# Linear attention into two feed-forward networks: moving one down product per chunk by a unit, and one tile of output products into the tail

## The chip, the cores and the metric

The program runs on one core of a Trainium2 chip, in one launch. The metric is device time in microseconds (us): the median of several runs. The engines are called as the profile calls them: PE is TensorE (PEld its weight load), DVE is VectorE, ACT is ScalarE, POOL is GpSimd, SP is SyncE, which here issues nearly all DMA transfers. Each engine works through its own instructions in a fixed order; an instruction that waits holds up all that stand behind it on that engine.

## The reference

Three steps, one feeding the next:

```python
for t in range(S):                       # attention: B=4, H=8, S=768, D=48
    state = alpha[:, :, t, :, None] * state + k_t v_t^T
    y[:, :, t] = q_t state
x = y as (3072, 384)
h = x @ w_in                             # first network, (3072, 384) @ (384, 2048)
g = (a0 + a1 h + a2 h^2 + a3 h^3) / (1 + |b0| |h| + |b1| h^2 + 1e-6)
x = g @ w_out                            # (3072, 2048) @ (2048, 384)
h = x @ w_in2                            # second network, (3072, 384) @ (384, 1024)
s = h * softmax(h)
out = (layernorm(s) * g_ln) @ w_out2     # (3072, 1024) @ (1024, 384)
```

All inputs and outputs are float32.

## The kernel before, in words

**Chunks and units.** The sequence is cut into six chunks of 128 steps (512 tokens with the four batches). A chunk is 16 units of the first network, one for each block of 128 of the 2048 hidden features; unit u belongs to chunk u // 16. The loop over u runs through 96 units and four more (`LAG = 4`). In it `m_up(u)` (line 592) makes the up products of a unit, nine matmuls into a PSUM tile `hp` (three buffers), and hands them to a chain on ACT, DVE and POOL that ends in `gh` (ACT, line 625) and `gl` (POOL, line 626), the high and low part of g, with two buffers each. `m_down(u - LAG)` (line 638) follows in the same round and adds that unit's nine down products into three PSUM tiles `x2p`, which collect a whole chunk. After a chunk's last unit ACT copies the three `x2p` tiles out (`x2e`, line 646); the first down product of the next chunk writes the same PSUM tiles. The attention of later chunks (lines 236 to 494) is woven into these rounds.

**The second network** works on 24 tiles of 128 tokens, four to a chunk. For tile s, `n_up` (line 712) makes 18 matmuls into a PSUM tile `h`; DVE and ACT then compute softmax, product and layer norm (lines 731 to 750), and DVE transposes blocks of the result (line 752). After the fourth tile of a chunk `n_turn` (line 762) completes the transposition by 16 transfers issued from SP, called turn transfers below. `n_split(s)` makes the high part (ACT, line 767) and the low part (POOL, or DVE for tiles 0 and 20, line 768) of one transposed tile in one of three places. `n_down(s)` (line 776) makes 24 matmuls into a PSUM tile `op` with two buffers, so tile s uses the buffer of tile s - 2. `n_out(s)` copies `op` on ACT into an SBUF tile `o` (line 785), also with two buffers, and four transfers of 32 rows, called output pieces below, carry it to the result (line 788, SP; for the last tile two of them from ACT).

**The order.** The first four tiles of the second network go into the last chunk of the first. The loop over tiles 4 to 23 then makes one tile's up products and norm, then one earlier tile's split, down products and output, except after the tiles named in `SKIP`; `done` counts the down products made, `cut` the splits, at most `AHEAD = 3` beyond `done`. What is left over goes into a last loop, the tail. Before the change 17 tiles of down products (0 to 16) are made in the loop and 7 in the tail.

```python
        while cut < min(done + AHEAD, (s + 1) // B * B):
            n_split(cut)
            cut += 1
        if s not in SKIP:
            n_out(done, n_down(done))
            done += 1
```

The program's scheduler takes the instructions in this order and settles, from priorities and its own model of durations, the order on each engine; waits between engines are semaphores. A second copy of both networks, for inputs that the fast form can't treat, stands behind a branch and isn't run here.

Of the kernel before, what the change touches and what calls it, by code (L numbers as in the profile page):

```python
# [23 lines left out]
def _run(*gens):  # L24
    for g in gens:
        for _ in g:
            pass
# [3 lines left out]
def kernel(  # L31
# [17 lines left out]
    B, H, S, D = q.shape  # L49
# [4 lines left out]
    NCH = S // CH  # L54
# [7 lines left out]
    LAG = 4  # L62
# [15 lines left out]
    G2 = 3  # L78
    MIX = lambda u: u < 24 and u % 2 == 0
    EARLY = (9, 11, 13, 15)  # L80
    SKIP = (5, 7, 11)
    AHEAD = 3
    LATE = 2
    U2, IDLE = NF1 - 1, (0, NF1 // 2 - 1)
    assert (B, H, D, CH) == (4, 8, 48, 128)
# [57 lines left out]
    def judge(moe_pool):  # L143

        sums = const.tile([128, 1], F32, name="sums")
        row = moe_pool.tile([1, 128], F32, name="row", tag="ft", bufs=2)
        tot = const.tile([1, 1], F32, name="tot")
        nc.vector.tensor_reduce(sums, bad, axis=AX.X, op=ALU.add)
        nc.sync.dma_start(out=row, in_=sums)
        nc.vector.tensor_reduce(tot, row, axis=AX.X, op=ALU.add)  # L150
        nc.vector.tensor_scalar(flag, tot, 0.0, None, ALU.is_gt)

    def network(fast):
# [420 lines left out]
        def x_load(c):  # L574
            for kt in range(KT):
                nc.sync.dma_start(
                    out=x_tile(c)[:, kt].rearrange("p a t -> p (a t)").bitcast(F32), in_=y_d[c][128 * kt:128 * kt + 128, :]
                )
# [50 lines left out]
        def m_down(u):  # L629
            c, f = divmod(u, NF1)  # L630
            n, o = divmod(f, 4)
            if f == 0:
                x2ps[c] = [ps_x2p.tile([128, NTOK], F32, name=f"x2p{d}", tag=f"x2p{d}") for d in range(KT)]
            gh, gl = gts.pop(u)
            hi, lo = wo[n]
            for d in range(KT):
                for w, gg in ((hi, gh), (hi, gl), (lo, gh)):
                    nc.tensor.matmul(  # L638
                        x2ps[c][d], lhsT=w[:, o, 128 * d:128 * d + 128], rhs=gg,
                        start=(f == 0 and w is hi and gg is gh), stop=(f == NF1 - 1 and w is lo),  # L640
                    )
            if f == NF1 - 1:
                for d0, n in ((0, 2), (2, 1)):
                    e = moe_pool.tile([128, 2, NTOK], F32, name="x2e", tag="st", bufs=2)
                    for d in range(n):
                        nc.scalar.activation(e[:, d], x2ps[c][d0 + d], AF.Copy, scale=back if fast else 1.0)  # L646
                    nc.sync.dma_start(out=x2_d[c][:, d0:d0 + n, :], in_=e[:, :n])
                del x2ps[c]
# [14 lines left out]
        def w2_load(nm):  # L663
            src = {"i": w2i_d, "o": w2o_d}[nm]
            n, step = {"i": (KT, 1), "o": (NF2, 4)}[nm]
            for z in range(0, n, step):
                for x, y in enumerate("hl"):
                    nc.sync.dma_start(out=w2[nm + y][:, z:z + step].bitcast(F32), in_=src[:, x, z:z + step])
                    yield
# [12 lines left out]
        def open2():  # L682
            if fast:
                ps_a.__exit__(None, None, None)
            ph2["ps_pool"] = tc.tile_pool(name="ps_e", bufs=1, space=PSUM, side="right", reuse_waits="tile")
            ph2["ps"] = ph2["ps_pool"].__enter__()
            if fast:
                att.__exit__(None, None, None)
            ph2["pool"] = tc.tile_pool(name="w2", bufs=1, side="right", reuse_waits="tile")
            pool = ph2["pool"].__enter__()  # L690
            for nm, dims in (("i", [128, KT, DF2]), ("o", [128, NF2, DM])):
                for y in "hl":
                    w2[nm + y] = pool.tile(dims, F32R, name="w2" + nm + y)
# [3 lines left out]
        def room(n, o, size):  # L697
            if n not in area:
                area[n] = moe_pool.tile([128, GW], F32R if n == 3 else F32, name=f"room{n}", tag=f"g{n}")
            return area[n][:, o:o + size]  # L700
# [56 lines left out]
        def n_turn(c):  # L757
            T = room(c % 2, 0, 4 * DF2).rearrange("p (r x) -> p r x", r=4)
            for qq in range(4):
                L = lnT[4 * c + qq] = room(2, DF2 * ((4 * c + qq) % 6), DF2)  # L760
                for r in range(4):
                    nc.sync.dma_start(out=L[32 * r:32 * r + 32, :], in_=T[32 * qq:32 * qq + 32, r])  # L762

        def n_split(s):
            L = lnT[s]
            hi, lo = (room(3, DF2 * (3 * x + s % 3), DF2) for x in range(2))
            nc.scalar.activation(hi, L, AF.Copy)  # L767
            (nc.vector if s in FASTS else nc.gpsimd).tensor_tensor(lo, L, hi.bitcast(F32), ALU.subtract)  # L768
            lnT[s] = (hi, lo)
# [32 lines left out]
        def chain(*gens):  # L802
            for g in gens:
                yield from g
# [48 lines left out]
        def half_steps(i):  # L853
            gp = a_pe(i)
            gd = chain(a_prep(i + 1), a_move_qk(i + 1) if i + 1 >= NPE else iter(()), a_load(i + 2, ("ra", "rk")) if i + 2 < NH and i + 1 >= NPE else iter(())) if i + 1 < NH else iter(())
            while True:
                with pin(GP):
                    a = next(gp, "end")
                with pin(GS):
                    b = next(gd, "end")  # L860
                    if b != "end":
                        b = next(gd, "end")
                if a == "end" and b == "end":
                    if i + 1 < NH:
                        _run(a_enter(i + 1))
                        if i + 2 < NH and i + 1 < NPE:
                            _run(a_load(i + 2))
                    return
                yield
# [2 lines left out]
        side = iter(())  # L872
        tail = None
        prep = iter(())
        for u in range(NU + LAG):
            c, f = divmod(u, NF1)
            now[0] = u
            if f % (NF1 // 2) == LATE and u < NU:
                _run(side)
                i = 2 * c + 2 + f // (NF1 // 2)  # L880
                side = half_steps(i) if fast and i < NH else iter(())
            if u < NU:
                if f == 0 and c == NCH - 1:
                    if fast:
                        judge(moe_pool)
                    open2()
                    tail = chain(w2_load("i"), n_load(0), w2_load("o"))
                if f == 0 and c and not fast:
                    x_load(c)
                if fast and u < NF1:  # L890
                    if f % 4 == 0:
                        _run(prep)
                        if f:
                            stage["near"] = False
                            stage["bank"] = ""
                        prep = w1_group(f // 4 + 2) if f < 8 else iter(())
                    with later(G1):
                        take(prep, 1)
                m_up(u)
                if fast and u < NF1:  # L900
                    with later(G1):
                        take(prep, 1)
            if u == NU:
                _run(n_load(1))
            take(side, 1)
            if u >= U2 and f % (NF1 // 2) in IDLE:
                stage["bank"] = "at"
                with later(G2):
                    take(split2, 1)
            if tail is not None:  # L910
                _run(split2)
                take(tail, 2)
            if u >= LAG:
                m_down(u - LAG)
            if u - NU + NF1 in EARLY:
                n_tile(EARLY.index(u - NU + NF1))
                if len(EARLY) == B and u - NU + NF1 == EARLY[-1]:
                    n_turn(0)
# [7 lines left out]
        done = 0  # L926
        cut = 0
        for s in range(len(EARLY), NS):
            if s % B == 0 and 1 < s // B + 1 < NCH:
                _run(n_load(s // B + 1))  # L930
            n_tile(s)
            if s % B == B - 1:
                n_turn(s // B)
            while cut < min(done + AHEAD, (s + 1) // B * B):
                n_split(cut)
# [4 lines that stand above are left out]
        while done < NS:  # L940
            while cut < min(done + AHEAD, NS):
                n_split(cut)
# [117 lines left out]
```

## Time and profile before

| | us |
|---|---|
| median of 3 runs | 779.71 |
| lowest, highest | 774.92, 781.45 |
| profiled execution, whole time | 776.87 |
| profiled execution, span of its instructions | 775.0 |
| PE busy | 728.0 |
| DVE busy | 630.4 |
| ACT busy | 535.2 |

The profiled execution took 1.87 us more than its span (776.87 less 775.0), and lies inside the range of the runs. Busy times are sums over stages that have different limits, so a stage is read by itself below. All times of single instructions are counted from the start of the span.

### The profile page before, as it was taken

How to read it: one execution, taken by the hardware profiler on the slowest of the kernel's cores; microseconds unless marked ns; L12 is line 12 of the kernel's file. 1: busy time of each engine (PE TensorE's matmuls, PEld its weight loads, DVE VectorE, ACT ScalarE, POOL GpSimd, SP SyncE). 2: the span in 40 equal slices, each digit the busy share in tenths (PEclk: the TensorE clock that was granted, in tenths of full speed). 3: DMA queues.
4: the chain of work that ended last, by engine and by line, in shares of the span. 5: the costliest groups of instructions: out<-in, count | busy, mean ns of one | idle time of the engine just before them, and what ended most of it. 6: DMA issues, size and time to landing. Idle time of an engine off the chain costs nothing.

```text
span 775.0 us, 13914 instructions
## 1 busy us (share of the span) xinstructions
PE 728.0 (94%) x4976; PEld 605.8 (78%) x4976; DVE 630.4 (81%) x1110; ACT 535.2 (69%) x983; POOL 358.4 (46%) x306
## 2 busy tenths in 40 slices
PE   4676999999999999999999999999999999999996
PEld 3565767788888787778877788888888989988986
DVE  4999999989898989899898966478887788877640
ACT  2245867689878888788878887788965545555541
POOL 3255777777554355434444433332243343452322
PEclk9857899999999999999999999999999999999999
DMA  7995446466837382727554350720025253542653
GB/s 167 253 275 165 107 155 167 146 147 206 204 99 161 122 205 83 172 66 207 137 148 91 124 82 1 296 112 0 1 83 132 89 130 90 132 108 52 140 119 76
DMA packets 87278, 101.74 MB, mean 131 GB/s; under 512 B 34464, under 2 KB 63136, under 8 KB 87200
## 3 DMA queue, kind: packets, MB, share of 16 engines
q1 hardware_dynamic: 87104, 100.67, 48.9%
q8 instruction: 41, 0.67, 0.4%
q14 instruction: 37, 0.30, 0.1%
q10 hardware_dynamic: 96, 0.10, 0.0%
HBM read 60.59 MB, written 27.56 MB: 114 GB/s over the span
## 4 chain that ended last, share of the span: by engine, by line
DVE 30%; PE 18%; ACT 12%; issue 5%; SPq 3%; DMA 3%; POOL 1%; ACTq 0%; DVEq 0%; POOLq 0%
PE x2p L638 6%; PE hp L592 6%; DVE room L752 3%; SPq L762 3%; DVE room L735 2%; DVE p L618 2%; ACT jk L737 2%; PE op L776 2%; DVE hp L622 2%; DVE w L621 2%; DMA room<-room 2%; DVE sm L731 2%; DVE room L750 2%; PE h L712 2%; DVE p L623 2%
## 5 line engine op out<-in xcount | busy, mean ns | idle before, releaser
L592 PE MATMUL hp<-xt,g 128*128 128x512 f32 x864 | 224.1, 401 | 14.8 <-DVE p L616 7.5
L626 POOL TENSOR_TENSOR gl<-p,gh 128x512 fp32r<-128x512 f32 x96 | 130.8, 1362 | 193.9 <-ACT gh L625 107.9
L592 PEld LDWEIGHTS hp<-xt,g 128*128 128x128 f32 x864 | 163.2, 192 | 54.2 <-DVE p L616 7.7
L638 PE MATMUL x2p<-gh,g 128*128 128x512 f32 x576 | 196.9, 395 | 2.0 <-ACT x2e L646 2.0
L638 PEld LDWEIGHTS x2p<-gh,g 128*128 128x128 f32 x576 | 107.9, 188 | 29.1 <-ACT x2e L646 4.7
L638 PE MATMUL x2p<-gl,g 128*128 128x512 f32 x288 | 112.9, 392 | 0.0
L776 PE MATMUL op<-w2oh,room 128*128 128x384 f32 x384 | 101.8, 339 | 1.3 <-ACT room L767 0.7
L768 POOL TENSOR_TENSOR room<-room,room 128x1024 fp32r<-128x1024 f32 x22 | 54.8, 2496 | 101.0 <-ACT room L767 79.0
L621 DVE SCALAR_TENSOR_TENSOR w<-w,co,hp 128x512 f32<-128x512 f32 x84 | 62.0, 738 | 43.5 <-ACT hp L620 42.5
L712 PE MATMUL h<-w2ih,x 128*128 128x512 f32 x288 | 90.7, 394 | 0.0
L599 ACT ACTIVATE p<-hp,co 128x512 f32<-128x512 f32 x96 | 66.0, 687 | 12.3 <-POOL gl L626 12.0
L620 ACT ACTIVATE hp<-ah 128x512 f32<-128x512 f32 x84 | 50.1, 597 | 33.3 <-DVE p L618 32.0
L776 PEld LDWEIGHTS op<-w2oh,room 128*128 128x128 f32 x384 | 70.1, 188 | 3.0 <-ACT room L767 1.0
L600 ACT ACTIVATE w<-ah,co 128x512 f32<-128x512 f32 x96 | 69.4, 724 | 1.7 <-DVE hp L622 1.3
L618 DVE SCALAR_TENSOR_TENSOR p<-p,co,hp 128x512 f32<-128x512 f32 x84 | 61.6, 734 | 9.3 <-ACT p L599 9.0
L597 ACT ACTIVATE ah<-hp 128x512 f32<-128x512 f32 x96 | 56.7, 591 | 16.4 <-PE hp L592 16.0
L776 PE MATMUL op<-w2ol,room 128*128 128x384 f32 x192 | 65.0, 339 | 0.0
L625 ACT ACTIVATE gh<-p 128x512 fp32r<-128x512 f32 x96 | 59.9, 623 | 5.7 <-DVE p L623 2.8
L638 PEld LDWEIGHTS x2p<-gl,g 128*128 128x128 f32 x288 | 54.1, 188 | 11.7 <-issue 0.8
L712 PEld LDWEIGHTS h<-w2ih,x 128*128 128x128 f32 x288 | 53.9, 188 | 11.7
L623 DVE SCALAR_TENSOR_TENSOR p<-p,co,hp 128x512 f32<-128x512 f32 x84 | 61.9, 737 | 1.1
L619 ACT ACTIVATE ah<-w,co 128x512 f32<-128x512 f32 x84 | 60.6, 721 | 1.3
(168 smaller groups left out, 1264.7 us busy)
## 6 DMA issues: line engine op xcount, KB each, us to landing
room<-room SPq DMA_DIRECT2D x96, 128.0 KB, 2.3
qk_d<-qk SPq DMA_DIRECT2D x10, 771.0 KB, 4.1
st<-in_moe_w_in_dram SPq DMA_DIRECT2D x13, 512.0 KB, 4.6
st<-in_moe_w_out_dram SPq DMA_DIRECT2D x16, 384.0 KB, 3.5
qks<-qk_d SPq DMA_DIRECT2D x20, 257.0 KB, 4.4
x<-x_d SPq DMA_DIRECT2D x18, 256.0 KB, 3.1
out_dram<-o SPq DMA_DIRECT2D x94, 48.0 KB, 1.6
ra<-in_alpha_dram SPq DMA_DIRECT2D x44, 96.0 KB, 2.8
```

Of the source, the lines that this page charges most:

```text
L592: last["PE", u] = nc.tensor.matmul(hp, lhsT=w[:, kt, 128 * o:128 * o + 128], rhs=xts[c][:, kt, xx, :], start=(kt == 0 and w is hi and xx = ...
L599: nc.scalar.activation(p, hp, AF.Square, bias=co[:, 7:8])
L600: nc.scalar.activation(w, ah, AF.Square, bias=co[:, 6:7])
L618: nc.vector.scalar_tensor_tensor(p, p, a1, hp, ALU.add, ALU.mult)
L619: nc.scalar.activation(ah, w, AF.Ln, bias=rest)
L621: nc.vector.scalar_tensor_tensor(w, w, rest, hp, ALU.add, ALU.mult)
L623: fin[u] = nc.vector.scalar_tensor_tensor(p, p, a0, hp, ALU.add, ALU.mult)
L625: last["ACT", u] = nc.scalar.activation(gh, p, AF.Copy)
L626: last["POOL", u] = nc.gpsimd.tensor_tensor(gl, p, gh[:].bitcast(F32), ALU.subtract)
L638: nc.tensor.matmul(x2ps[c][d], lhsT=w[:, o, 128 * d:128 * d + 128], rhs=gg, start=(f == 0 and w is hi and gg is gh), stop=(f == NF1 - 1 an ...
L712: nc.tensor.matmul(hp[:, 512 * n:512 * n + 512], lhsT=x2s[c][:, kt, x, CH * b:CH * b + CH], rhs=w2[w][:, kt, 512 * n:512 * n + 512], start ...
L776: nc.tensor.matmul(op, lhsT=x[:, 128 * f:128 * f + 128], rhs=w2[w][:, f, :], start=(f == 0 and x is hi and w == "oh"), stop=(f == NF2 - 1 ...
```

## The change

It has two parts. With `HOLD` the list `held` keeps the down products of the first unit of chunks 2, 3 and 4 back by one round: in that round only the up products are put down, in the next one both down products follow one another. With 15 in `SKIP` no down products are made after tile 15, so from tile 16 on every tile's down products stand one tile later, 16 tiles of them are made in the loop and 8 in the tail. A new inner loop makes the splits that are still due for the chunks before, ahead of the turn transfers that overwrite their source.

```diff
-    SKIP = (5, 7, 11)
+    SKIP = (5, 7, 11, 15)
     AHEAD = 3
+    HOLD = (1, NCH - 1)
...
+        held = []
         for u in range(NU + LAG):
...
             if u >= LAG:
-                m_down(u - LAG)
+                held.append(u - LAG)
+            if not (f == LAG and HOLD[0] < c < HOLD[1]):
+                while held:
+                    m_down(held.pop(0))
...
             n_tile(s)
             if s % B == B - 1:
+                while cut < min(done + AHEAD, s // B * B):
+                    n_split(cut)
+                    cut += 1
                 n_turn(s // B)
```

Eight lines are added ahead of the code named here, so the same instruction has a line number higher by one in the rows of after.

On PE, at the start of chunk 2 (the tile `x2p` has three parts, and `sc` is the attention's; chunks 3 and 4 read alike), there stood:

```order
L592 MATMUL hp<-xt,g_629 128x512 x7
L420 MATMUL sc<-qks 128x128 x8
L592 MATMUL hp<-xt,g_629 128x512 x2
L638 MATMUL x2p_3026<-gh,g_134 128x512
L638 MATMUL x2p_3026<-gl,g_134 128x512
L638 MATMUL x2p_3026<-gh,g_134 128x512
L638 MATMUL x2p_3027<-gh,g_134 128x512
L638 MATMUL x2p_3027<-gl,g_134 128x512
L638 MATMUL x2p_3027<-gh,g_134 128x512
L592 MATMUL hp<-xt,g_629 128x512 x9
```

and now, on PE at the same place:

```order
L593 MATMUL hp<-xt,g_629 128x512 x7
L421 MATMUL sc<-qks 128x128 x8
L593 MATMUL hp<-xt,g_629 128x512 x11
L639 MATMUL x2p_3061<-gh,g_134 128x512
L639 MATMUL x2p_3061<-gl,g_134 128x512
L639 MATMUL x2p_3061<-gh,g_134 128x512
L639 MATMUL x2p_3062<-gh,g_134 128x512
L639 MATMUL x2p_3062<-gl,g_134 128x512
```

The nine up products of the next unit moved ahead of the first down products of the chunk.

On SP, over the last three chunks of the second network (`room` is a turn transfer, `out_dram` an output piece, four to a tile), there stood:

```order
L762 DMA room_6225<-room_6208 32x1024 x16
L788 DMA out_dram<-o 32x384 x16
L762 DMA room_6225<-room_5889 32x1024 x16
L788 DMA out_dram<-o 32x384 x20
L762 DMA room_6225<-room_6208 32x1024 x16
L788 DMA out_dram<-o 32x384 x22
```

and now, on SP at the same place:

```order
L763 DMA room_6225<-room_6208 32x1024 x16
L789 DMA out_dram<-o 32x384 x12
L763 DMA room_6225<-room_5889 32x1024 x16
L789 DMA out_dram<-o 32x384 x19
L763 DMA room_6225<-room_6208 32x1024 x16
L789 DMA out_dram<-o 32x384 x27
```

Counted back from the end (tile 23 has two pieces on SP, the others four), the pieces behind the last 16 turn transfers were those of tiles 18 to 23; now they are the fourth piece of tile 16 and all of tiles 17 to 23.

On ACT, from the last tile's layer norm (lines 745 and 746) to the end, there stood:

```order
L745 ACTIVATE sm<-sm 128x1
L746 ACTIVATE sm<-sm 128x1
L785 ACTIVATE o<-op 128x384 x2
L767 ACTIVATE room_6352<-room_6225 128x1024
L785 ACTIVATE o<-op 128x384
L767 ACTIVATE room_6352<-room_6225 128x1024 x3
L785 ACTIVATE o<-op 128x384 x4
```

and now, on ACT at the same place:

```order
L746 ACTIVATE sm<-sm 128x1
L747 ACTIVATE sm<-sm 128x1
L768 ACTIVATE room_6352<-room_6225 128x1024
L786 ACTIVATE o<-op 128x384 x2
L768 ACTIVATE room_6352<-room_6225 128x1024 x3
L786 ACTIVATE o<-op 128x384 x2
L768 ACTIVATE room_6352<-room_6225 128x1024
L786 ACTIVATE o<-op 128x384 x4
```

Before, these were outputs 17 and 18, split 20, output 19, splits 21 to 23, outputs 20 to 23; now they are split 19, outputs 16 and 17, splits 20 to 22, outputs 18 and 19, split 23, outputs 20 to 23.

## Rows read from the trace of the kernel before

**Rows 1.** The page: span, and busy time of each engine.
```profile
span 775.0 us, 13914 instructions
PE 728.0 (94%) x4976; PEld 605.8 (78%) x4976; DVE 630.4 (81%) x1110; ACT 535.2 (69%) x983; POOL 358.4 (46%) x306
```
**Rows 2.** Windows: length; busy PE, PEld, DVE, ACT, POOL; granted clock, DMA share, GB/s.
```profile
262.00:440.00 178.00, 173.41 (x1418) 137.75 (x1419) 162.28 (x264) 147.65 (x270) 83.27 (x78) 1.00 0.54 142
440.00:565.00 125.00, 124.71 (x718) 102.06 (x717) 88.18 (x135) 103.22 (x183) 39.62 (x34) 1.00 0.26 83
565.00:749.70 184.70, 184.70 (x910) 165.11 (x908) 138.84 (x271) 102.30 (x199) 71.57 (x38) 1.00 0.42 106
```
**Rows 3.** Waits of PE from 200 to 450: total, times, longest, in us.
```profile
PE x2p L638 <- ACT x2e L646: 2.0, 6, 0.5
...
PE hp L592 <- DVE p L623: 0.4, 2, 0.2
```
**Rows 4.** Waits of ACT from 262 to 440 (the longest two of four).
```profile
ACT hp L620 <- DVE p L618: 19.2, 11, 3.2
ACT p L599 <- POOL gl L626: 5.5, 9, 1.0
```
**Rows 5.** Waits of ACT from 450 to 565 (the longest of eight).
```profile
ACT ah L597 <- PE hp L592: 9.5, 9, 3.0
```
**Rows 6.** Timeline of PE, start of chunk 2: start, us, idle before and its releaser.
```profile
261.88 0.50 PE L638 MATMUL x2p<-gh,g 128*128 128x512 f32 x1 [0.43 <-ACT x2e L646]
...
263.07 0.50 PE L638 MATMUL x2p<-gh,g 128*128 128x512 f32 x1 [0.23 <-ACT x2e L646]
```
**Rows 7.** Timeline of PE, end of tile 19's down products to the last matmul.
```profile
749.55 0.34 PE L776 MATMUL op<-w2oh,room 128*128 128x384 f32 x1
750.60 0.45 PE L776 MATMUL op<-w2oh,room 128*128 128x384 f32 x1 [0.71 <-ACT room L767]
...
751.86 0.62 PE L776 MATMUL op<-w2oh,room 128*128 128x384 f32 x2 [0.64 <-DVE room L768]
...
768.39 0.33 PE L776 MATMUL op<-w2oh,room 128*128 128x384 f32 x1
```
**Rows 8.** Timeline of ACT: outputs 18 and 20, and split 20.
```profile
745.68 0.49 ACT L785 ACTIVATE o<-op 128x384 f32<-128x384 f32 x1 [2.76 <-PE op L776]
749.49 1.06 ACT L767 ACTIVATE room<-room 128x1024 fp32r<-128x1024 f32 x1 [3.31 <-DMA room<-room]
...
759.44 0.49 ACT L785 ACTIVATE o<-op 128x384 f32<-128x384 f32 x1 [0.24 <-DMA out_dram<-o]
```
**Rows 9.** Timeline of SP's queue: the last turn transfers and the pieces behind them.
```profile
745.25 10.87 SPq L762 DMA_DIRECT2D room<-room  x16
756.21 13.90 SPq L788 DMA_DIRECT2D out_dram<-o  x22
```
**Rows 10.** Timeline of DVE: a step of tile 15, then steps of tile 23.
```profile
681.42 2.07 DVE L747 TENSOR_TENSOR sm<-sm 128x1 f32<-128x1 f32 x1 [0.50 <-ACT sm L746]
...
741.84 0.15 DVE L744 TENSOR_SCALAR sm<-sm 128x1 f32<-128x1 f32 x1 [1.31 <-ACT jk L737]
742.50 0.16 DVE L747 TENSOR_TENSOR sm<-sm 128x1 f32<-128x1 f32 x1 [0.50 <-ACT sm L746]
...
743.93 1.25 DVE L752 STREAM_TRANSPOSE room<-room 128x1024 f32<-128x1024 f32 x1
```
**Rows 11.** Timeline of POOL: the low part of tile 11.
```profile
681.07 2.40 POOL L768 TENSOR_TENSOR room<-room,room 128x1024 fp32r<-128x1024 f32 x1
```
**Rows 12.** Windows, columns as in rows 2.
```profile
75.90:82.70 6.80, 3.46 (x8) 2.78 (x9) 6.77 (x14) 5.21 (x10) 4.86 (x5) 0.50 0.74 128
```
**Rows 13.** Timeline of PE: nine up products before and after a pause.
```profile
68.30 2.33 PE L592 MATMUL hp<-xt,g 128*128 128x512 f32 x9
...
79.24 3.94 PE L592 MATMUL hp<-xt,g 128*128 128x512 f32 x9 [7.55 <-DVE p L616]
```
**Rows 14.** The page's DMA issues: count, KB each, median us to landing.
```profile
out_dram<-o SPq DMA_DIRECT2D x94, 48.0 KB, 1.6
```

## The prediction

> **What bounds the kernel now.** I read the page first, then windows by stage, then the waits inside each stage, and the timelines at the places that the change touches. The page gives PE 728.0 us of a span of 775.0 [rows 1], but that average hides three stages. From 262 to 440 PE is busy 173.4 of 178 us [rows 2] and yet it isn't what sets the pace: in the waits of ACT no PE appears, the longest are for DVE and POOL [rows 4], so the chain of ACT, DVE and POOL runs behind PE, and PE is held by the buffers that the chain gives back. From 440 to 565 it is the other way: PE is busy 124.7 of 125 us [rows 2] and ACT waits for up products, 9.5 us in nine waits [rows 5]. From 565 to 749.7 PE is busy all of 184.7 us [rows 2]. Beside it the second network's norm runs as a chain of its own on DVE and ACT, a few tiles behind the up products; both streams meet at the end. PE ends tile 19 just after 749.55, waits 0.71 and then 0.64 us for the two halves of tile 20, and has nothing but down products from 751.86 to 768.39 + 0.33 = 768.72 [rows 7]. From there to the end it is 775.0 - 768.72 = 6.28 us of last output, which nothing here changes.
>
> **Part 1, the held down product.** Nothing is added or removed, 27 matmuls change places. At the start of chunk 2 PE waits 0.43 and 0.23 us, because ACT hasn't yet copied out the `x2p` tiles [rows 6]; the six waits of this kind are two at each of the three starts that are changed, 2.0 us in all [rows 3]. Nine up products (2.0 to 2.3 us, [rows 13]) now stand ahead and cover them. That is at most 2.0 us of PE's time. But at chunks 2 and 3 the chain on ACT and DVE sets the pace, and what PE saves there it spends waiting for the next `hp` buffer, except that the moved products also let ACT and DVE take some steps earlier. Chunk 4 starts at about 430, ten us ahead of the stage in which PE has no slack, so most of its 0.66 us should reach the end. The moved up products need an `hp` buffer 2.6 us earlier than before; PE has waited for those 0.4 us in total over 250 us [rows 3], so I bound the loss by 0.4. I take a gain of 1.0, between a loss of 0.4 and a gain of 2.0.
>
> **Part 2, one tile more in the tail: PE's own work.** All up products from tile 16 on stand one tile of down products earlier on PE, and all down products one tile later relative to them. The sum of PE's work ahead of tile 20 is the same, in another order, and PE has no idle time up to 749.7, so it arrives at tile 20 at the same time as before. Up products that come earlier help DVE only where DVE waits for them, and it waits for ACT. So this part gives PE nothing by itself; what it can change is when tile 20 is ready.
>
> **Part 2, the end of the norm's chain.** Let T be the end of the last transposition, before at 743.93 + 1.25 = 745.18 [rows 10]. DVE's own order changed around tiles 15 to 18, where two tiles are now interleaved twice. Each tile alone leaves DVE idle for 1.31 + 0.50 us behind ACT [rows 10], so two interleavings can save at most 2 x 1.81 = 3.6 us. Against it, the splits now fall at other moments of the chain, and a step of DVE that begins inside POOL's subtraction is held until that ends: at 681.42 a step of one element a row, elsewhere 0.16 us, took 2.07 us, to the end of the 2.40 us subtraction that began at 681.07 [rows 10, 11]. One such meeting more costs up to 2.4. So T moves between -3.6 and +2.4; I take -0.5, since following the new order by hand through the four tiles I get a gain of one interleaving and lose most of it to one meeting.
>
> **Part 2, the output pieces behind the turn transfers.** This is the largest term. Before, all pieces of tiles 0 to 17 were issued ahead of the last 16 turn transfers; now the fourth piece of tile 16 and those of 17 stand behind them on SP. The 16 take SP 10.87 us from T + 0.07, and the next piece was issued at 756.21, T + 11.0 [rows 9]. It lands 1.6 us later [rows 14], at T + 12.6. Who waits: output 18 on ACT writes the `o` buffer that this piece still reads (two buffers, tiles 16 and 18 share one). Before, the same kind of wait fell on output 20, 0.24 us at 759.44 [rows 8], where it cost nothing. Behind it on PE: tile 20's first matmul writes the `op` buffer that output 18 has to empty. Before, output 18 ran at 745.68 [rows 8], long ahead; now it runs from T + 12.6 to T + 13.1 (0.49 us, [rows 8]). PE starts tile 20 some 0.06 us later (749.49 + 1.06 = 750.55 on ACT, 750.60 on PE, [rows 7, 8]), at T + 13.2 = 758.4 for T unchanged. The 94 matmuls from 751.86 on took 16.86 us, 0.179 each, so 96 take 17.2 and end at 775.6, against 768.72: **+6.8 us**. The two waits of 0.71 and 0.64 us disappear inside this one and are in the sum. Bounds of the landing: output 20 began 3.2 us after the first of the four pieces that it waited for was issued [rows 8, 9], so one piece takes 1.6 to 3.2 us, and I take the median of its own kind. The pieces are 48 KB. The Trainium skill ("DMA: Bandwidth & Descriptors", Anatomy of one DMA) states for the GpSimd path a fixed cost of about 2.0 us and bytes at 436 GB/s, which is an estimate of 2.1 us by that page; by it the sum would be 0.5 us higher, but the trace has 1.6 for this very transfer and decides.
>
> **The clock after the pause.** PE would then stand idle from tile 19's end (749.7, or a little later) to 758. After the pause of 7.55 us ahead of 79.24 the granted clock was 0.50, the lower level of 1.2 GHz, from 75.9 to 82.7 [rows 12], and nine up products took 3.94 instead of 2.33 us [rows 13]. I add these 1.6 us, between nothing (no fall) and 3.4 (the whole stretch of 6.8 us at half speed falls on work).
>
> **The sum.** 6.8 - 0.5 + 1.6 - 1.0 = +6.9 us. The profiled execution would go from 776.87 to 783.8. The median of the runs shown is 2.84 higher than that execution, so on it the forecast is 779.71 + 6.9 = **786.6 us**, slower by 0.9%. A measurement of this kernel can tell about 1%, 7.8 us, from no change; the forecast lies just inside.
>
> **Rival 1, the pause closes and the change is not slower.** The tile that was left for the tail keeps PE busy until tile 20 is ready. Its price: tile 20 would follow tile 19 at 749.73 and the last 96 matmuls end at 749.73 + 17.2 = 766.9, 1.8 us earlier; with 1.0 to 2.0 from part 1 that is some 2.8 to 3.8 us faster, about 776.5. It decides if the fourth piece of tile 16 lands by 749.1, that is if T comes 8.7 us earlier, or if ACT doesn't wait for it. The order shows the piece behind the transfers, and 3.6 is all that interleaving can save. 4%.
>
> **Rival 2, T comes early and the clock holds.** 6.8 - 3.6 - 2.0 = +1.2, or 780.9. For it speaks that two interleavings are really in the order, against it the meetings with POOL, and the fall of the clock in every long pause at the start. 13%.
>
> **Rival 3, everything falls on the later side.** One more meeting on DVE, no saving (T + 2.4 at most; I take + 1.0), a landing of 2.4, a clock cost of 2.5 and no gain from part 1: 6.8 + 1.0 + 0.8 + 2.5 = +11.1, or 790.8. The turn transfers fill SP for 10.87 us in any case, so nothing here is more than an addition of small terms. 13%.
>
> **How the numbers follow.** The forecast (the blocked piece, with terms near those taken) has 70%. The cases by themselves: rival 1 at 776.5, rival 2 at 780.9, forecast 783.5 to 789.5, rival 3 at 790.8. The range 780.0 to 790.5 leaves out rival 1 and half of rival 3, and some of the spread of the median itself, whose runs reach from 774.92 to 781.45. Slower by over 1% takes rival 3 and a third of the forecast: 0.36. Faster by over 1% isn't reached even by rival 1 at its best: 0.02. The rest, 0.62, is within 1%.
>
> **What would show it.** In the waits of PE in chunks 2 to 4 the wait for `x2e` should be gone, and one for `hp` should have grown. In the last 35 us PE should stand idle 6 to 8 us ahead of tile 20, released by ACT's output 18, and that output in turn by the landing of an output piece, issued on SP right behind the last turn transfers. The clock should read 0.50 in a stretch that begins in that pause. If PE runs through from tile 19 to 20, or is released there by a split as before, the largest term is wrong. If the pause is there and the whole is no slower, part 1 gave more than PE's own waits, and my reading of the stage from 262 to 440 is wrong.

## The result, and the profile after

The changed kernel takes 783.72 us (median of ten runs, 782.53 to 787.53) against 777.36 for the kernel before on the same chip (ten runs, 773.78 to 781.45): ratio 1.0091, 95% interval 1.0068 to 1.0114. It is slower, by 0.9%, as forecast: +6.9 us was forecast, and the ratio gives 0.0091 x 777.36 = 7.1 us (the two medians are 6.4 us apart). The time on record as the forecast, 786.6 us, is 2.9 higher, because it starts from the median of three runs, 779.71, and that of ten is 777.36. The changed kernel's profiled execution took 783.25 us with this span and these busy times; PE's 3.5 us more than in [rows 1] are no more work, it has the same 4976 matmuls.

```profile
span 781.4 us, 13916 instructions
PE 731.5 (94%) x4976; PEld 608.5 (78%) x4976; DVE 630.2 (81%) x1110; ACT 534.2 (68%) x983; POOL 356.8 (46%) x306
```

**Chunks 2 to 4.** The waits of PE from 200 to 450 (total, times, longest), to be held against [rows 3] and against two more lines of before:

```profile
PE u L483 <- DVE xt L471: 1.8, 4, 0.7
PE y L444 <- POOL A L428: 0.9, 2, 0.6
```

and after:

```profile
PE u L484 <- DVE xt L472: 2.1, 4, 0.7
PE hp L593 <- DVE p L624: 1.6, 5, 0.5
PE y L445 <- POOL A L429: 0.9, 2, 0.6
```

The wait for `x2e` is gone (it was 2.0), the wait for an `hp` buffer has gone from 0.4 to 1.6, and that for `xt` from 1.8 to 2.1. All waits of PE in this stretch were 5.1 us and are 4.6.

**The tail.** From 565 on PE waits in two places, for one releaser:

```profile
PE op L777 <- ACT o L786: 6.2, 2, 6.0
```

The timeline of PE shows the longer one. The last matmul of tile 19 ends at 749.53 + 0.33 = 749.86, at nearly the same time as in [rows 7]; tile 20 begins 6 us later, in one wait where before there were two of 0.71 and 0.64, and PE ends at 774.88 against 768.72.

```profile
749.53 0.34 PE L777 MATMUL op<-w2oh,room 128*128 128x384 f32 x1
755.83 0.69 PE L777 MATMUL op<-w2oh,room 128*128 128x384 f32 x1 [5.97 <-ACT o L786]
...
774.55 0.33 PE L777 MATMUL op<-w2oh,room 128*128 128x384 f32 x1
```

Who holds output 18 stands in the timeline of ACT (against [rows 8]): split 22, then output 18, which waits 1.99 us for an output piece.

```profile
752.25 1.06 ACT L768 ACTIVATE room<-room 128x1024 fp32r<-128x1024 f32 x1 [1.85 <-DMA room<-room]
755.29 0.49 ACT L786 ACTIVATE o<-op 128x384 f32<-128x384 f32 x1 [1.99 <-DMA out_dram<-o]
```

So two things hold output 18, one behind the other: split 22, which needs the turn transfers and ends at 752.25 + 1.06 = 753.31, and then the piece, for the last 1.99 us. Which of them would be enough alone, this trace doesn't tell; twice_19, below, does.

On SP (against [rows 9]) that piece is the first of the 27 behind the last turn transfers:

```profile
742.52 10.14 SPq L763 DMA_DIRECT2D room<-room  x16
752.70 23.57 SPq L789 DMA_DIRECT2D out_dram<-o  x27
```

The chain that ended last (start, us, what) goes through the same places: DVE's last transposition, 16 turn transfers on SP (the first of them here), the landing of the piece, output 18, and 96 matmuls.

```profile
741.21 1.26 DVE room L753
742.52 0.51 SPq L763
...
752.70 2.51 DMA out_dram<-o
755.29 0.50 ACT o L786
755.83 19.07 PE op L777 x96
```

T, the end of the last transposition, is 742.46 here. Counted from it, the piece is issued at T + 10.24, lands at T + 12.75, output 18 begins at T + 12.83, tile 20 at T + 13.37. The windows show the clock (the last three numbers are granted clock, DMA share, GB/s; before, it was 1.00 from 749.7 to the end of PE's work):

```profile
749.90:753.10 3.20, 0.00 (x0) 0.00 (x0) 0.00 (x0) 1.34 (x2) 2.34 (x1) 1.00 0.90 204
753.10:759.90 6.80, 4.07 (x13) 4.07 (x14) 0.00 (x0) 1.18 (x3) 2.34 (x1) 0.50 0.45 110
```

The granted clock is at its lower level, 1.2 GHz, for 6.8 us that begin inside the pause; 4.07 us of it fall on matmuls. The last 96 take 774.88 - 755.83 = 19.05 us, 1.85 more than 17.2.

### The profile page after: what moved, and what is told of

Same layout as the page of the kernel before. It is cut to its first block, busy times and chain, and to the rows that moved or that the text cites. A ratio compares the mean times of both kernels' runs of the same rounds, so it can differ in the third digit from the quotient of the medians.

```text
span 781.4 us, 13916 instructions
## 1 busy us (share of the span) xinstructions
PE 731.5 (94%) x4976; PEld 608.5 (78%) x4976; DVE 630.2 (81%) x1110; ACT 534.2 (68%) x983; POOL 356.8 (46%) x306
## 4 chain that ended last, share of the span: by engine, by line
DVE 28%; PE 18%; ACT 12%; issue 6%; SPq 4%; DMA 3%; POOL 2%; ACTq 0%; DVEq 0%; POOLq 0%
PE x2p L639 6%; PE hp L593 6%; SPq L763 4%; DVE room L753 3%; PE op L777 2%; DVE room L736 2%; DVE p L619 2%; ACT jk L738 2%; DVE sm L732 2%; DVE hp L623 2%; DVE room L751 2%; DVE w L622 2%; PE h L713 2%; DMA room<-room 2%; DVE p L624 2%
## 5 line engine op out<-in xcount | busy, mean ns | idle before, releaser
L777 PE MATMUL op<-w2oh,room 128*128 128x384 f32 x384 | 103.5, 343 | 6.4 <-ACT o L786 6.2
```

What stands on the lines that cost most here:

```text
L777: nc.tensor.matmul(op, lhsT=x[:, 128 * f:128 * f + 128], rhs=w2[w][:, f, :], start=(f == 0 and x is hi and w == "oh"), stop=(f == NF2 - 1 ...
```

## The experiments

Theory A is the prediction's: an output piece behind the turn transfers holds output 18, and that holds PE. Theory B: eight tiles in the tail instead of seven cost PE time of their own. Theory C: the held down products disturb the chain of ACT and DVE. All ratios are to the kernel before, run beside them (its medians there are 777.64 to 777.94, so the ratios can be compared with one another better than the medians).

| kernel | median us (runs) | ratio, interval |
|---|---|---|
| hold_only | 778.97 (12) | 1.0004, 0.9979 to 1.0028 |
| skip_only | 784.83 (4) | 1.0080, 1.0051 to 1.0109 |
| act_pieces | 776.66 (12) | 0.9979, 0.9952 to 1.0005 |
| before_piece_late | 782.17 (10) | 1.0042, 1.0023 to 1.0060 |
| act_163 | 783.89 (8) | 1.0072, 1.0045 to 1.0100 |
| act_16 | 779.39 (10) | 1.0027, 1.0005 to 1.0049 |
| before_act_pieces | 778.15 (12) | 0.9993, 0.9967 to 1.0018 |
| skip_act | 777.49 (12) | 0.9992, 0.9968 to 1.0017 |
| pieces_first | 777.90 (12) | 0.9998, 0.9976 to 1.0021 |
| twice_19 | 782.11 (12) | 1.0058, 1.0034 to 1.0083 |

**One part alone: hold_only and skip_only.** The changed kernel with one of its two parts undone.

```diff
-    SKIP = (5, 7, 11, 15)          # hold_only
+    SKIP = (5, 7, 11)
...
-    HOLD = (1, NCH - 1)            # skip_only
+    HOLD = (NCH, 0)
```

> Part 1 alone: HOLD as changed, SKIP back to (5, 7, 11). Theory A (the fourth output piece of tile 16 stands behind the last turn transfers, output 18 waits for it, PE waits for output 18): nothing of that is here, so the time is that of the kernel before, less the little that part 1 gives, 0 to 1 us (ratio 0.999 to 1.000); the waits of PE for x2e in chunks 2 to 4 are gone and waits for hp buffers take their place. Rival B (8 tiles of down products in the tail instead of 7 cost 4.2 us of PE's time and a fall of the clock): the same. Rival C (the held down products disturb the chain on ACT and DVE, and that is the loss): slower by about 6 us, ratio 1.008.

> Part 2 alone: 15 in SKIP and the new inner loop, no down product held. Theory A: all of the loss, 6 to 7 us (ratio 1.008 to 1.009), with PE idle 6 us ahead of tile 20, released by output 18, and that by the landing of an output piece. Rival B: the same. Rival C: no loss, ratio 1.000.

The hold alone makes no difference that can be measured, and the skip alone has all of the loss: C falls. In the waits of PE from 200 to 450, hold_only shows that the edit did its work, and where the time went (1.8 and 0.4 without the hold):

```profile
PE u L484 <- DVE xt L472: 2.3, 5, 0.7
PE hp L593 <- DVE p L624: 1.5, 5, 0.5
```

**The pieces issued elsewhere: act_pieces, and its control before_act_pieces.** The output pieces of tiles 16 and 17 are issued by ACT; in the changed kernel, and in the kernel before.

```diff
-  (nc.scalar if s == NCH * B - 1 and b >= 2 else nc.sync).dma_start(...)
+  (nc.scalar if s in (16, 17) or s == NCH * B - 1 and b >= 2 else nc.sync).dma_start(...)
```

> The changed kernel with both parts; only the four output pieces of tiles 16 and 17 are issued from ACT instead of SP, so none of tile 16 or 17 stands behind the last turn transfers on SP. On ACT outputs 18 and 19 now stand ahead of splits 21 and 22. Theory A: PE runs from tile 19 into tile 20 without a pause, the clock doesn't fall, the 96 last matmuls end some 17.1 us after tile 19, 7 to 8 us earlier than in the changed kernel (ratio to the kernel before 0.997 to 0.999, against 1.009). Rival B: the eight tiles are still in the tail, so at least 4 us of the loss stay (1.005 or more). Rival C: no difference to the changed kernel, 1.009.

> The kernel before, with the output pieces of tiles 16 and 17 issued by ACT; a control for the run in which the changed kernel had these pieces there. In the kernel before these pieces stand ahead of the last turn transfers and hold nobody up. Theory A: no effect, ratio 0.998 to 1.002; then the 7 us that the same edit gave the changed kernel were the blocked piece alone. If the issue from ACT were a gain by itself (a shorter queue on SP, an earlier start of the turn transfers), this kernel too would be faster by 2 us or more.

The loss is gone with eight tiles still in the tail, so B falls; the control gains nothing, so what the edit gave the changed kernel wasn't the other queue by itself. The edit moved more than the pieces: on ACT outputs 18 and 19 now stand ahead of split 22, so neither the piece nor that split holds them. In the windows of act_pieces the last 97 matmuls stand without a gap, at full clock:

```profile
753.60:770.60 17.00, 17.00 (x97) 16.80 (x96) 0.00 (x0) 4.30 (x7) 7.17 (x3) 1.00 0.41 99
```

Two things in these traces are not part of the changed kernel's loss, but a reader should know them. In act_pieces PE stood idle earlier, 2.30 us ahead of tile 17, for ACT's output 15, and from 740 to 743 the granted clock was 0.51. The same wait is 2.30 in skip_only and 2.25 in act_163, and 0.2 to 0.4 in the other five kernels with 15 in `SKIP`, the changed kernel among them; so it comes and goes, and why isn't shown. And in the control PE ended tile 19 at 747.98, 1.9 us earlier than before, and waited 2.65 us for split 20.

**All on SP, in another order: pieces_first.** The same test without ACT's queue: the turn transfers of the last chunk are written down behind the outputs of tiles 16 and 17.

```diff
-                n_turn(s // B)
+                if s < NS - 1:
+                    n_turn(s // B)
...
         while done < NS:
+            if done == 18:
+                n_turn(NCH - 1)
```

> The changed kernel, with the last chunk's turn transfers written down later in the program, behind the outputs of tiles 16 and 17. All transfers stay on SP; on SP the order becomes 20 pieces, 2 turn transfers, 4 pieces, 14 turn transfers, 22 pieces, so that all pieces of tiles 16 and 17 are ahead of all but two turn transfers. It tells the place in SP's queue apart from what the issue from ACT may give. Theory A: the piece that holds output 18 is gone; 14 of the turn transfers start 4 x 0.42 = 1.7 us later, so the two halves of tile 20, which were complete 6.6 us after the last transposition, are complete after 8.3 us, about 750.8, against an end of tile 19 at 749.9. The pause shrinks from 6.0 to about 1 us, PE ends at about 768, the median falls by 6 to 7 us to 777 to 778, ratio to the kernel before 0.998 to 1.003. Theory B (eight tiles in the tail cost time of their own): 783 to 784 as before, or slower by the 1.7 us.

The loss is gone here too, and the two small waits of [rows 7] are back, 0.37 and 0.65 us, for splits again. Output 18 stands ahead of split 20 here (it begins at 746.72). SP and PE of pieces_first:

```profile
743.91 1.15 SPq L763 DMA_DIRECT2D room<-room  x2
745.15 1.92 SPq L789 DMA_DIRECT2D out_dram<-o  x4
747.12 9.66 SPq L763 DMA_DIRECT2D room<-room  x14
756.88 13.91 SPq L789 DMA_DIRECT2D out_dram<-o  x22
```

```profile
751.23 0.44 PE L777 MATMUL op<-w2oh,room 128*128 128x384 f32 x1 [0.37 <-ACT room L768]
...
752.49 0.62 PE L777 MATMUL op<-w2oh,room 128*128 128x384 f32 x2 [0.65 <-DVE room L769]
```

**Four pieces, and one: act_16 and act_163.** As act_pieces, for tile 16 alone, and for its fourth piece alone.

```diff
+  (nc.scalar if s == 16 or s == NCH * B - 1 and b >= 2 else nc.sync)            # act_16
+  (nc.scalar if (s, b) == (16, 3) or s == NCH * B - 1 and b >= 2 else nc.sync)  # act_163
```

> The changed kernel, with the four output pieces of tile 16 issued by ACT; tile 17's pieces stay on SP behind the turn transfers. Theory A: the o buffer of tile 17 is then the one that comes free late, so the output that waits for it, and with it the pause of PE, moves one tile on, from tile 20 to tile 21, and the pause is shorter by tile 20's work of 4.3 us: some 2 to 3 us instead of 6. PE ends at 770 to 772 of the span instead of 774.9, the median is 779 to 781. Theory B: no change, 783 to 784.

> The changed kernel, with one transfer moved: the fourth output piece of tile 16 is issued by ACT and not by SP. Nothing else differs; tile 17's pieces still stand behind the turn transfers. Theory A (the piece behind the turn transfers holds output 18, and that holds tile 20 on PE): output 18 is free of the transfers, so the pause of 6.0 us ahead of tile 20 shrinks by some 2 us; what is late next ahead of output 18 on ACT is split 22, which needs the last turn transfers, so a pause of some 4 us stays, now with split 22 ahead of output 18 and not the piece. The median falls by 1.5 to 3 us against the changed kernel, to about 781. Theory B (eight tiles in the tail cost PE time of their own): nothing changes, 783 to 784. If one piece were the whole of it, the pause would close and the median fall by 6 us.

act_16 came out at the time that A has. The pause moved to the first matmul of tile 21, and in the chain output 19 is released by a piece of tile 17 that was issued behind the turn transfers:

```profile
755.27 1.63 DMA out_dram<-o
...
756.97 0.50 ACT o L786
...
757.51 14.52 PE op L777 x72
```

But the piece lands at 755.27 + 1.63 = 756.90, and in the timeline of ACT split 23, which stands right ahead of output 19, ends at the same moment, 757.00. Either would have held output 19 until then, so this run agrees with A and doesn't tell the piece from the split:

```profile
755.94 1.06 ACT L768 ACTIVATE room<-room 128x1024 fp32r<-128x1024 f32 x1 [1.62 <-DMA room<-room]
756.97 0.49 ACT L786 ACTIVATE o<-op 128x384 f32<-128x384 f32 x1
```

act_163 didn't do what it was made for. With the fourth piece gone from SP, the scheduler put another piece of the same tile behind the turn transfers; 18 pieces stand between the last two batches now (19 in the changed kernel), and 27 behind the last, as in the changed kernel:

```profile
725.48 17.81 SPq L789 DMA_DIRECT2D out_dram<-o  x18
743.93 10.15 SPq L763 DMA_DIRECT2D room<-room  x16
754.13 23.92 SPq L789 DMA_DIRECT2D out_dram<-o  x27
```

So it can't tell one piece from four. It is a repetition of the changed kernel instead, with nearly the same time, and its chain has the same links: the piece, then output 18, then PE.

```profile
754.13 2.31 DMA out_dram<-o
756.46 0.50 ACT o L786
...
757.01 19.68 PE op L777 x96
```

**The block alone, in the kernel before: before_piece_late.** Only the fourth piece of tile 16 is issued later, behind the last turn transfers.

```diff
-  nc.sync.dma_start(out=L[32 * r:32 * r + 32, :], in_=T[32 * qq:32 * qq + 32, r])
+  marks["turn"] = nc.sync.dma_start(out=L[32 * r:32 * r + 32, :], in_=T[32 * qq:32 * qq + 32, r])
...
+  with tc.issue_after(marks["turn"].ins) if (s, b) == (16, 3) and fast else ExitStack():
```

> The kernel before, without either part of the change; one single output piece, the fourth of tile 16 (48 KB), is issued behind the last 16 turn transfers. Seven tiles in the tail as before. Theory A: output 18 waits for that piece until about 12.7 us after the last transposition, and since splits 20 to 22 stand behind output 18 on ACT here, PE starts tile 20 later still; with the fall of the clock 9 to 13 us slower (ratio 1.012 to 1.017). Rivals B and C: no loss, ratio 1.000, since neither the tail's length nor the order of the down products is changed.

It is slower, but by less than expected, and not by the route that was expected. The scheduler answered the late piece by another order on ACT: output 18 began at 745.47, before the late piece was even issued (754.89), so it didn't wait for it, and output 19 went behind all four splits. In the chain, split 23 and not the piece is what output 19 ran behind:

```profile
754.25 2.78 DMA room<-room
757.18 0.95 ACT room L767
758.67 15.56 PE op L776 x72
```

So this run shows only that a late piece costs here; not that it costs by the wait itself.

**With and without the hold, where nothing swallows it: skip_act.** act_pieces with `HOLD = (NCH, 0)`.

> The changed kernel without the held down products, and with the output pieces of tiles 16 and 17 issued by ACT: eight tiles in the tail, nothing blocked, no hold. Theory A, in which the hold gives nothing measurable (at most 0.2 us at the end): the same as with the hold, ratio to the kernel before 0.996 to 1.001, within 1.5 us of the version with the hold. If the hold is worth the 1.0 us that was forecast or more, it shows here, where PE has no pause that swallows it: 1 us slower than with the hold. Theory B: 783 to 784 as for the changed kernel.

No difference that can be measured: 0.9992 against 0.9979, each +/- 0.0026.

**The pause filled with work: twice_19.** PE makes the down products of tile 19 twice.

```diff
-            for f in range(NF2):
+            for f in [*range(NF2)] * (2 if s == 19 else 1):
```

> The changed kernel, in which PE makes the 24 down products of tile 19 twice over, into the same PSUM tile (the second time starts again from nought, so the output is the same): 4.3 us more work, put where PE stands idle. It measures the clock term by itself. Theory A: tile 20 starts as before 13.1 to 13.4 us after the last transposition, since output 18 doesn't wait for PE; the pause shrinks from 6.0 to about 1.7 us, and 4.3 us of work more cost nothing. If the pause of 6 us is what takes the clock down, the last 96 matmuls take 17.2 us in place of 19.06, and the median falls by up to 1.9 us against the changed kernel, to 781.9; if a pause of 1.7 us is enough for that, it stays at 783.7. Theory B, in which PE's own work in the tail sets the end: 4.3 us slower, 788.

24 more matmuls cost nothing that can be measured: B falls once more. The pause shrank to 1.85 us, and output 18, in the timeline of ACT, now waited 5.00 us for the piece, since here it stands ahead of split 22 (the second row). So the piece alone is enough to hold output 18, and this is the run that shows it:

```profile
753.41 0.49 ACT L786 ACTIVATE o<-op 128x384 f32<-128x384 f32 x1 [5.00 <-DMA out_dram<-o]
753.80 1.05 ACT L768 ACTIVATE room<-room 128x1024 fp32r<-128x1024 f32 x1
```

The clock term didn't go away. The windows show full clock up to 752, and 0.63 behind the short pause; the last 96 matmuls took 772.71 - 753.96 = 18.75 us, 1.5 over 17.2.

```profile
749.00:752.00 3.00, 3.00 (x18) 2.79 (x16) 0.00 (x0) 0.00 (x0) 1.88 (x1) 1.00 0.90 205
...
756.40:759.40 3.00, 3.00 (x13) 3.00 (x12) 0.00 (x0) 0.00 (x0) 0.89 (x1) 0.63 0.33 84
```

## Why the prediction was right

**The blocked piece (+6.8) was the right mechanism, and nearly the right size.** It rests on one number, tile 20's start counted from T, forecast T + 13.2. Four kernels have a piece of tile 16 behind all 16 turn transfers and output 18 waiting for it:

| kernel | T | tile 19 ends on PE | tile 20 begins | begins - T |
|---|---|---|---|---|
| after | 742.46 | 749.86 | 755.83 | 13.37 |
| skip_only | 742.39 | 749.80 | 755.69 | 13.30 |
| act_163 | 743.87 | 752.42 | 757.01 | 13.14 |
| twice_19 | 740.47 | 752.11 | 753.96 | 13.49 |

Whatever PE did before, tile 20 began 13.1 to 13.5 us after T. Where the pieces were moved out of the way, it began behind tile 19 or behind its splits. The prediction left one thing out: in the first three of these kernels split 22 stands ahead of output 18 on ACT. In the changed kernel it ends at 753.31, and output 18 is followed by tile 20 after 0.54 us, so by that order alone, with no late piece, PE would have waited until about 753.85, some 4.0 of the 5.97 us (an estimate from these rows). It doesn't change the sum, since the piece lands later than the split and holds output 18 by itself in twice_19, to the same distance from T. But by the same estimate, taking the piece out and leaving the order on ACT would have won back only about 2 us. With T unchanged the term is 745.18 + 13.37 + 17.2 - 768.72 = 7.0. Inside it two sizes were off and cancelled, which was luck: SP's turn transfers gave the next piece its issue at T + 10.24 and not T + 11.0, and that piece took 2.51 us to land (2.31 to 2.71 in the other three kernels), against the median of 1.6 that was taken; all lie inside the bounds of 1.6 to 3.2. Why the 16 transfers took SP 10.14 us here and 10.87 before isn't shown. The 2.1 us estimated from the Trainium skill ("DMA: Bandwidth & Descriptors", Anatomy of one DMA, for the GpSimd path) lies between: this piece took longer than that estimate, the median of its kind less.

**T (-0.5, between -3.6 and +2.4) was taken too small.** T itself differs by up to 4.8 us between executions (740.47 to 745.24), since the whole second network begins earlier or later. Its distance from the transposition of tile 11 doesn't. In the changed kernel these two rows of DVE are 89.73 us apart:

```profile
651.48 1.24 DVE L753 STREAM_TRANSPOSE room<-room 128x1024 f32<-128x1024 f32 x1
...
741.21 1.25 DVE L753 STREAM_TRANSPOSE room<-room 128x1024 f32<-128x1024 f32 x1
```

With 15 in `SKIP` it is 89.69 to 89.78 in all eight kernels, without it 91.12 to 91.20 in all four (the kernel before: 652.78 to 743.93, 91.15). So the new order on DVE moves T by -1.4: of the at most 3.6 us that two interleavings could save, 40% is left in the end. All of it arises between the transpositions of tiles 14 and 18, 30.10 us apart in place of 31.55. From 676 to 706 DVE's waits for ACT fell from 7.3 to 6.4 us, and where it had met POOL's subtraction once, in a step of 2.07 us, it now met it twice, in steps of 0.77 and 2.27. These don't add up to 1.4, so what made the rest stays open. The prediction also says too much of such meetings: not every step is held. In the kernel before, the step of L735 at 702.07 took its usual 1.28 us inside a subtraction that ran from 701.87 to 704.27.

**The clock (+1.6) was 1.85.** The fall and its place were right. That the size came so near is partly luck: it was taken from one pause in another stage, and pauses in these kernels cost 1.5 to 2.6 us. That one as short as 1.85 us can bring nearly the same cost was not foreseen (below).

**The hold (-1.0, between +0.4 and -2.0) gave nothing that can be measured.** Three pairs with and without it stand at 1.0004 against 1, 1.0091 against 1.0080, and 0.9979 against 0.9992. Two of the three lean to a loss and one to a gain, all by less than the intervals. The step that failed is "most of its 0.66 us should reach the end" with the lead that ACT and DVE were to gain: in the trace the 2.0 us of waits for `x2e` came back as 1.2 us of waits for `hp` and 0.3 for `xt`, and the rest, 0.5, is less than the runs can tell. At chunk 4, which was to give the gain, it is the same: from 425 to 565 PE waited 0.7 for `x2e` and 0.3 for `xt` before, and 0.5 for `hp` and 0.4 for `xt` after, so 0.1 was left. The moved up products met an `hp` buffer that wasn't free, beyond the loss of 0.4 that the prediction allowed for it. This agrees with the reading that PE isn't what sets the pace from 262 to 440.

**The sum.** 7.0 - 1.4 + 1.85 + 0 = 7.45, against 6.9 forecast and 7.1 measured (6.4 by the medians). The errors of T (-0.9) and of the hold (+1.0) cancelled by luck, so the total is better than its parts. In the two profiled executions PE's end moved by 6.16; the missing 1.3 is the earlier transposition of tile 11 (651.48 against 652.78), the kind of difference that executions of one kernel have.

Rival 1 (the pause closes) is what the changed kernel would have been without the blocked piece and without split 22 ahead of output 18: act_pieces stands at 0.9979, about 1.6 us faster than before with an interval that reaches 1.0005, and not the 2.8 to 3.8 that the rival promised, of which 1.0 to 2.0 were the hold's. Its mechanism, a tail tile that covers the last splits, is there in the traces of act_pieces and skip_act, where PE runs from tile 19 to 20 without a gap. It can be worth about the 1.35 us of the two waits in [rows 7], less what the earlier wait ahead of tile 17 takes; that it is worth this isn't shown, as no version measured here is faster than the kernel before beyond its interval. A third `o` buffer would test the wait most directly; it wasn't tried.

## What to carry to other kernels

Leaving one more piece of work for the tail moves its transfers too: count on every issuing queue what now stands behind a long batch, and follow which buffer each late transfer still reads. Here a small transfer behind 16 large ones held, through two double buffers, an engine two steps away, which stood idle for 6 us. Measure such a block as a time from the event that starts the batch: here it was 13.1 to 13.5 us in four variants, and filling the pause with other work was free but didn't end it sooner. And read the order on every engine again after each edit: the scheduler answered the move of one transfer by moving others (act_163, before_piece_late), and more than one instruction can be holding the same one.

## What was not expected of the hardware

**The clock's cost hardly follows the length of the pause.** Ahead of the last tiles PE stood idle (times in us), and the matmuls behind it took longer than the same number at full clock (0.179 us each):

| kernel | pause | matmuls behind it | over |
|---|---|---|---|
| twice_19 | 1.85 | 96 in 18.75 | 1.5 |
| act_16 | 2.53 | 72 in 14.52 | 1.6 |
| before_act_pieces | 2.65, soon 0.65 more | 94 in 18.43 | 1.6 |
| before_piece_late | 3.19 | 72 in 15.55 | 2.6 |
| act_163 | 4.59 | 96 in 19.67 | 2.5 |
| skip_only | 5.89 | 96 in 18.99 | 1.8 |
| after | 5.97 | 96 in 19.05 | 1.85 |

The longest pause isn't the dearest, because part of the slow stretch then falls into the pause itself: in the changed kernel 6.8 - 4.07 = 2.73 us of it, while in act_163 the granted clock over the whole pause, 752.5 to 757, is still 0.85. Nor does a pause of a given length always bring a fall: behind the wait of 2.30 us ahead of tile 17 the clock was 0.54 from 739.26 to 742.75 in act_pieces, and behind the same wait of 2.30 us in skip_only (below) it stayed at 1.00 from 737 to 749. Behind the two waits of 0.71 and 0.64 us in the kernel before, and of 0.37 and 0.65 in pieces_first, the granted clock stayed at 1.00.

```profile
736.41 0.44 PE L777 MATMUL op<-w2oh,room 128*128 128x384 f32 x1 [2.30 <-ACT o L786]
```

**A small transfer lands later behind large ones.** 48 KB right behind 16 transfers of 128 KB took 2.51 us to land in the changed kernel, and 2.44, 2.31 and 2.71 in skip_only, act_163 and twice_19, where the fourth piece of tile 17 in act_16, three pieces further back, took 1.63 and the median is 1.6.

The Trainium skill ("DMA: Bandwidth & Descriptors", Queues, rings and completion order) states that the signal of a transfer's completion comes only behind all earlier writes of the same DMA engine; these times agree with it, and no run here tested it by itself.
